# Queueing the output weight's splits, one batch's slot inputs and the joined products behind a chain that others wait for

## The chip, the cores and the metric

The kernel runs on 1 core of one Trainium2 chip. The metric is the device time of one execution in microseconds (us); lower is better. The engines are PE (TensorE, matrix products), DVE (VectorE), ACT (ScalarE), POOL (GpSimd) and SP (the queue that issues most DMAs); they run side by side, each in its own order, and wait for each other by semaphores.

## What is computed

Three parts follow each other on 4608 tokens (8 batches of 576) of width 512. `x` of a part is the output of the part before it.

```python
# 1: attention, 8 heads of 64, softmax over blocks at or before one's own block of 64
x = softmax(mask(q @ k.T / 8)) @ v
# 2: soft mixture of 8 experts with 4 slots each
logits = x @ phi                                   # 4608 x 32
slot_input = softmax(logits, over tokens).T @ x    # 32 x 512
slot_out[e] = relu(slot_input[e] @ w1[e]) @ w2[e]
x = softmax(logits, over slots) @ slot_out
# 3: bilinear layer
out = ((x @ m2_w1) * (x @ m2_w2)) @ m2_w3 @ m2_w_out
```

## The kernel before

**Attention** (class `Attn`) works on 32 pairs of heads, four to a batch. The order of its instructions on all engines comes from a planner (`Plan`), which gives each operation a duration, a due time and the operations that it waits for; `Attn.run` (L770) writes them out in that order. While it runs, POOL, DVE and ACT also unpack pieces of the bilinear layer's weights (`background`); the output weight `w_out` then lies in the tile `wO`. Of each batch's 576 tokens the planner also makes the logits, the combine weights (`cT`, which go to the array `cs` in memory by `cTd`) and that batch's share of the slot inputs (`S`, added up in `SS` by `SSu`).

**The tail of attention** (`push_tail`, L600) does the same for the last batch, out of the planner. It is a list of small steps: logits (L630), their transposes (L639) and scaling on DVE (L642, L645), natural-order tokens (`x_nat`, L682, L684), the softmax over tokens (`disp_max`, L689 and the exponentials L545 to L555), its transposes (L698), the sum over all batches (`slot_sum`: `tot` L719, its transpose L721, and a chain of eight operations on one partition, L726 to L733), the slot inputs (`slot_in`, L577, L579, L706), the scale `rl` (`slot_share`, L738, L740) and the transposed, scaled slot inputs `siT` (`slot_T`, L710 to L714). Between them stand small products of zeros (`warm`, L45), which only keep PE busy. With `siT` the experts can begin.

**The experts and the joined weight** (`Rest.run`). Since `m2_w3 @ m2_w_out` doesn't depend on the tokens, it is computed as one matrix `W` of 1024 x 512 in 192 joined products (L908), which are put between the experts' steps in portions: `MM[k]` says how many go out at step k, and the last call, step `STEPS` = 28, sends out all that are left. For each product both factors are split into a high and a low part (`split`, L862): a cast to the high part, and a subtraction for the low part. For `wO` and the first two pieces of `w3` (`convert(0)`, `convert(1)`) both are done on POOL; for the other fourteen pieces of `w3`, which are unpacked by four DVE operations (`narrow`, L808 to L816) and one of ACT (L812), the cast is ACT's and the subtraction POOL's. An expert e takes its first layer (L993, tile `h`), a copy `hs` by ACT (L1002), two transposes `hTp` (L1011), the rectified copy by ACT (L1012) and its second layer (L1021, tile `so`).

**The factors' chain.** After the last expert: copy `so`, sum and transpose it (`sumT`, L950), multiply by `m2_w1` and `m2_w2` (`ab`, L1062), copy, transpose (`abT`, L1069) and copy again (L1076). From these two factors DVE and ACT make the products of slot pairs in eight groups (L1088 to L1096, tile `g_stage`), and POOL one small part (L1099 to L1101); PE multiplies them by `W` (L1110, L1116) into `H` (L1120). **The final stage** (`final`) multiplies pairs of combine weights by `H`: 36 tiles of 13 matmuls (L1213, L1215).

In `Attn.run` the order of the planner's operations is kept as written. From `push_tail` on, a scheduler orders each engine's instructions, except in the manual region from the experts on, where PE's and SP's order is as written; `tc.issue_after(x)` keeps what is inside from being put ahead of x. The lines around the change:

```python
self.tail.extend([*logits[:2], sum_t, *logits[2:], *lts, *(F(x_late, c) for c in range(3)), F(fill, 1), disp_max, F(x_late, 3), F(x_late, 4),
                  F(fill, 2), disp_nat, slot_sum, F(fill, 3), slot_in, slot_share, F(fill, 4), slot_T, F(fill, 5)])
```

## Time and profile before

| | |
|---|---|
| three timed runs | 603.77 us median (602.77 to 604.93) |
| the profiled execution | 603.69 us, span of its instructions 601.9 us |
| PE busy | 573.4 us (95% of the span) |
| DVE, ACT, POOL busy | 396.2, 318.7, 343.3 us |
| granted PE clock, mean over the span | 0.971 |

The profile is of one execution. A stretch (start:end, in us from the first instruction) has the busy time of each engine, the share of full speed that PE's clock was granted, and the share of time that the DMA engines were busy. A row of a timeline has the start, the time taken, the engine, the line of the kernel, the operation, the tile that is written <- the tiles that are read, and in brackets how long the engine stood idle before it and whose result it then waited for. A matmul of unsplit 32-bit values (L630, L993, L1021) shows as two in the trace, one of split values (L908, L1110, L1213) as one. The attention part ends at about 343 us, the tail at 369, the experts at 444, the factors' chain at 456, and the final stage begins at 489.

### The profile page before, as it was taken

Reading aid. Unit: us, or ns where it says so; the run is one execution under the profiler, and the core shown is the slowest. Engines: PE = TensorE matmul, PEld = TensorE weight load, DVE = VectorE, ACT = ScalarE, POOL = GpSimd, SP = SyncE. Lnnn points to the kernel's source line nnn. Section 1 sums busy time; section 2 is a strip of 40 time slices with the busy share of each in tenths; the row PEclk is TensorE's granted clock in tenths of the full one; section 3 lists DMA queues with packets and bytes.
Section 4 is the critical chain, followed back from the end, with each engine's and each line's share of the span. In section 5 each row is a group of like instructions: output and inputs, shape, how many; then the busy total and the mean of one; then the engine's idle time right before and its main releaser. Section 6 shows DMA issues by size and latency. Waiting matters only on the chain.

```text
span 601.9 us, 13924 instructions
## 1 busy us (share of the span) xinstructions
PE 573.4 (95%) x5467; PEld 421.6 (70%) x5467; DVE 396.2 (66%) x701; ACT 318.7 (53%) x615; POOL 343.3 (57%) x256
## 2 busy tenths in 40 slices
PE   6999999999999999999999959999996999999997
PEld 3777777777777777776777635556562778888885
DVE  5648769788788798797884276735416995564550
ACT  4556477586675784874865522432532265445351
POOL 6587987878859969878768490411542032133230
PEclk8699999999999999999999987999997999999999
DMA  7243683754555647447436556999943026657642
GB/s 244 81 158 103 207 306 101 237 165 141 169 194 164 184 143 227 148 132 231 132 112 219 206 220 247 399 429 423 423 167 107 1 85 192 207 173 246 200 145 105
DMA packets 41113, 116.96 MB, mean 194 GB/s; under 512 B 7244, under 2 KB 17468, under 8 KB 38984
## 3 DMA queue, kind: packets, MB, share of 16 engines
q1 hardware_dynamic: 40868, 116.00, 56.1%
q8 instruction: 43, 0.70, 0.5%
q14 instruction: 22, 0.18, 0.1%
q10 hardware_dynamic: 180, 0.07, 0.0%
HBM read 105.75 MB, written 10.45 MB: 193 GB/s over the span
## 4 chain that ended last, share of the span: by engine, by line
PE 82%; DVE 9%; DMA 3%; ACT 3%; issue 2%; POOL 0%; ACTq 0%; DVEq 0%; POOLq 0%; SPq 0%
PE sc L371 18%; PE ops L1213 17%; PE pv L404 14%; PE wps L908 8%; PE sc L331 5%; PE pv L420 4%; PE h L993 3%; PE so L1021 2%; PE pv L528 2%; DVE bm L335 2%; DMA raw<-in_moe_w 2%; DMA raw<-in_qk 1%; PE ops L1215 1%; PE pv L471 1%; PE pv L577 1%
## 5 line engine op out<-in xcount | busy, mean ns | idle before, releaser
L335 DVE TENSOR_REDUCE bm<-sc 128x10 f32<-128x640 f32 (+2 forms) x128 | 122.5, 987 | 24.1 <-PE sc L331 20.3
L371 PE MATMUL sc<-set 64*128 64x320 f32 (+4 forms) x1152 | 116.8, 311 | 0.8 <-ACT PTa L379 0.3
L319 POOL TENSOR_TENSOR set<-raw,set 128x1152 fp32r<-128x1152 f32 x32 | 84.9, 2655 | 32.4 <-ACT set L312 31.0
L371 PEld LDWEIGHTS sc<-set 64*128 64x128 f32 x1152 | 90.7, 189 | 10.3 <-issue 3.8
L1213 PE MATMUL ops<-H,Ph 128*128 128x512 f32 x288 | 90.7, 395 | 0.9 <-DVE H L1120 0.9
L1188 POOL TENSOR_TENSOR Pl<-rot,Ph 128x384 fp32r<-128x384 f32 x24 | 31.0, 1311 | 92.5 <-ACT Ph L1186 92.5
L389 POOL TENSOR_TENSOR acc<-PTa,PTb 128x640 f32<-128x640 f32 x32 | 49.7, 1554 | 32.2 <-ACT PTb L379 25.0
L1213 PEld LDWEIGHTS ops<-H,Ph 128*128 128x128 f32 x288 | 54.3, 189 | 14.7 <-DVE H L1120 1.3
L371 PE MATMUL sc<-shift 64*128 64x320 f32 (+4 forms) x384 | 59.7, 305 | 0.0
L1213 PE MATMUL ops<-H,Pl 128*128 128x512 f32 x144 | 56.9, 395 | 0.0
L331 PE MATMUL sc<-set 64*128 64x320 f32 (+4 forms) x384 | 47.4, 330 | 4.1 <-ACT set L312 2.5
L1216 ACT COPY o<-ops 128x512 f32<-128x512 f32 x36 | 21.0, 587 | 57.0 <-PE ops L1215 56.7
L908 PE MATMUL wps<-wo,w 128*128 128x512 f32 x192 | 50.8, 406 | 0.0
L389 POOL TENSOR_TENSOR acc<-acc,PTc 128x640 f32<-128x640 f32 x31 | 48.2, 1556 | 2.4
L379 ACT ACTIVATE PTa<-sc 128x1024 f32<-128x1024 f32 x32 | 32.8, 1025 | 30.8 <-PE sc L371 28.3
L379 ACT ACTIVATE PTc<-sc 128x640 f32<-128x640 f32 (+1 forms) x64 | 41.7, 652 | 11.1 <-PE sc L371 10.2
L908 PEld LDWEIGHTS wps<-wo,w 128*128 128x128 f32 x192 | 34.1, 188 | 16.8 <-issue 10.8
L867 POOL TENSOR_TENSOR w<-f,w 128x512 fp32r<-128x512 f32 x14 | 18.1, 1290 | 46.7 <-ACT w L866 40.5
L404 PE MATMUL pv<-PTc,v 128*64 128x256 f32 (+1 forms) x256 | 44.0, 422 | 0.4 <-ACT xT L532 0.2
L462 POOL TENSOR_TENSOR xT<-xT,shift 128x576 f32<-128x576 f32 x28 | 39.0, 1422 | 3.9 <-DMA shift<-rr 3.7
L413 ACT COPY xT<-pv 128x256 f32<-128x256 f32 (+1 forms) x64 | 25.2, 397 | 28.2 <-PE pv L408 23.1
L379 ACT ACTIVATE PTb<-sc 128x1024 f32<-128x1024 f32 x32 | 32.8, 1024 | 11.3 <-PE sc L371 10.0
(248 smaller groups left out, 1133.1 us busy)
## 6 DMA issues: line engine op xcount, KB each, us to landing
win<-in_moe_w SPq DMA_DIRECT2D x16, 2048.0 KB
raw<-in_qk SPq DMA_DIRECT2D x32, 576.0 KB
v<-in_v SPq DMA_DIRECT2D x32, 320.0 KB
rot<-cs SPq DMA_DIRECT2D x48, 192.0 KB
out<-o SPq DMA_DIRECT2D x11, 768.0 KB
raw<-in_moe_w SPq DMA_DIRECT2D x16, 512.0 KB
shift<-rr SPq DMA_DIRECT2D x56, 144.0 KB
w3raw<-in_w3T SPq DMA_DIRECT2D x14, 512.0 KB
```

The costliest lines, as they stand in the source:

```text
L319: self.nc.gpsimd.tensor_tensor(lo, self.raw.pop(n), hi.bitcast(F32), op=ALU.subtract)
L331: self.nc.tensor.matmul(ps[:, h, o:o + kn], lhsT=qh[r, q0:q0 + 128], rhs=kh[r, k0:k0 + kn], start=True, stop=True)
L335: self.nc.vector.tensor_reduce(self.bmb[n % 2][:, :, o:o + m // 64], self.st.pop(("M", n, i))[:, :, 0:m].rearrange("p h (n k) -> p h n k", ...
L371: self.nc.tensor.matmul(ps[:, h, o0:o0 + w], lhsT=lt[r, k] if i < 3 else lt[r], rhs=rt[r, q0:q0 + w], start=i == 0, stop=i == 3)
L379: self.nc.scalar.activation(out=out, in_=ps[:, :, 0:sum(g[3] for g in self.UNITS[u])], func=AF.Exp, scale=SCALE)
L389: eng.tensor_tensor(acc[:, :, lo:hi], a, b, op=ALU.add)
L404: mm(ps[64 * h:64 * h + 64, q0 - lo:q1 - lo], lhsT=v[:, 128 * j + 64 * h:128 * j + 64 * h + 64], rhs=pt[:, h, o:o + q1 - q0], start=j == 0 ...
L413: self.nc.scalar.copy(self.xTb[b % 2][:, p, lo:hi], self.st.pop(("V", n, part))[:, 0:hi - lo])
L462: self.nc.gpsimd.tensor_tensor(x, x, self.rb[:, i], op=ALU.mult)
L908: nc.tensor.matmul(p, lhsT=a[:, o], rhs=b, start=c + i == 0, stop=c == 7 and i == 2)
L1188: eng.tensor_tensor(Pl[:, k], p, Ph[:, k].bitcast(F32), op=ALU.subtract)
L1213: nc.tensor.matmul(ps, lhsT=a[:, k, r], rhs=b[:, k], start=n == 0, stop=False)
```

## The change

It has three parts, besides line numbers that grow by up to four behind them.

1. The steps `S`, `SSu`, `cT`, `cTc` and `cTd` of the next-to-last batch are no longer written out where the planner puts them, but collected in `self.late` and written out in the tail behind the three steps that transpose and scale the last batch's logits (`lts`).
2. The splits of `wO` and of the first two pieces of `w3` wait for the copy of `rl` (`keep["shared"]`), the cast is ACT's instead of POOL's (`early` is gone), and each piece of `w3` is split ahead of the four pieces of `wO` that it meets.
3. `MM` changes at steps 21 and 24 to 27: the sum of all portions is 178 instead of 192, so that 14 joined products are left for the last call, which stands behind the factors' copies (L1076).

```diff
--- before.py
+++ after.py
@@ -32,7 +32,7 @@
 HP = False
 CT = (1, 2)
 STEPS = 28
-MM = (0, 5, 4, 13, 5, 4, 14, 5, 4, 13, 5, 4, 14, 5, 4, 13, 5, 4, 14, 5, 4, 13, 5, 4, 14, 4, 4, 4)
+MM = (0, 5, 4, 13, 5, 4, 14, 5, 4, 13, 5, 4, 14, 5, 4, 13, 5, 4, 14, 5, 4, 14, 5, 4, 2, 2, 4, 3)
 EPS = 1e-9
 
 SP = 640
@@ -241,7 +241,7 @@
         self.keep = keep
         self.raw, self.v = {}, {}
         self.m, self.mt, self.PT, self.acc, self.st = {}, {}, {}, {}, {}
-        self.tail = deque()
+        self.tail, self.late = deque(), []
 
         self.ident = keep["ident"]
         self.bmb = [self.const.tile([128, 2, 45], F32, name=f"bm{i}") for i in range(2)]
@@ -737,7 +737,7 @@
             ps = pst("rl")
             nc.tensor.matmul(ps[:, 0:1], lhsT=st["w"], rhs=ident[0:1, 0:1], start=True, stop=True)
             st["rl"] = tl([128, 1], "rl")
-            nc.scalar.copy(st["rl"], ps[:, 0:1])
+            self.keep["shared"] = nc.scalar.copy(st["rl"], ps[:, 0:1]).ins
 
         F = lambda f, *a: (lambda: f(*a))
         logits = [F(logit, g, i) for g in range(2) for i in range(2)]
@@ -750,7 +750,8 @@
             if WARM[i]:
                 warm(nc, self.keep, pst("warm"), WARM[i])
 
-        self.tail.extend([*logits[:2], sum_t, *logits[2:], *lts, *(F(x_late, c) for c in range(3)), F(fill, 1), disp_max, F(x_late, 3), F(x_late, 4),
+        late = [F(getattr(self, "op_" + name), n, slot) for name, n, slot in self.late]
+        self.tail.extend([*logits[:2], sum_t, *logits[2:], *lts, *late, *(F(x_late, c) for c in range(3)), F(fill, 1), disp_max, F(x_late, 3), F(x_late, 4),
                           F(fill, 2), disp_nat, slot_sum, F(fill, 3), slot_in, slot_share, F(fill, 4), slot_T, F(fill, 5)])
 
         def rest(tile, psum):
@@ -770,6 +771,9 @@
         self.constants()
         with self.tc.manual_schedule(engines={getattr(mybir.EngineType, e) for e in ORDERED}):
             for (name, n), slot, idle in Plan(self.nb).order():
+                if n == self.nb - 2 and name in ("S", "SSu", "cT", "cTc", "cTd"):
+                    self.late.append((name, n, slot))
+                    continue
                 if idle > .5 and name[0] in "MmQ" and n < 2:
                     warm(self.nc, self.keep, self.pv_b[slot] if name == "mT" else self.sc_b[slot][:, 0], int(4.5 * idle - 1), 256)
                 f = getattr(self, "op_" + name, None)
@@ -859,11 +863,8 @@
         self.nc.sync.dma_start(out=v, in_=self.io["moe_w1" if first else "moe_w2"][e].rearrange("p (c f) -> p c f", c=4 if first else 8))
         self.loaded.append(v)
 
-    def split(self, hi, lo, src, early=False):
-        if early:
-            self.nc.gpsimd.tensor_copy(hi, src)
-        else:
-            self.nc.scalar.copy(hi, src)
+    def split(self, hi, lo, src):
+        self.nc.scalar.copy(hi, src)
         self.nc.gpsimd.tensor_tensor(lo, src, hi.bitcast(F32), op=ALU.subtract)
 
     def run(self, out):
@@ -894,7 +895,7 @@
             def convert(i):
                 t = self.narrow(None, raws.pop(i), self.tmp, ps_u) if i > 1 else self.wO[:, 8 + i]
                 pair = w3_tile(i, F32R, "w3")
-                self.split(pair[:, 0:512], pair[:, 512:1024], t, i < 2)
+                self.split(pair[:, 0:512], pair[:, 512:1024], t)
                 pairs[i] = pair[:, 0:512], pair[:, 512:1024]
 
             def w_rows():
@@ -958,12 +959,13 @@
             for i in range(2, 2 * W3B):
                 load(i)
             done[0] = 2 * W3B
-            for c in range(8):
-                t = wo.tile([128, 1024], F32R, name=f"wo{c}")
-                wos.append((t[:, 0:512], t[:, 512:1024]))
-                self.split(*wos[c], self.wO[:, c], True)
-                if c % 4 == 0:
-                    convert(c // 4)
+            with tc.issue_after(keep["shared"]):
+                for c in range(8):
+                    if c % 4 == 0:
+                        convert(c // 4)
+                    t = wo.tile([128, 1024], F32R, name=f"wo{c}")
+                    wos.append((t[:, 0:512], t[:, 512:1024]))
+                    self.split(*wos[c], self.wO[:, c])
             done[1] = 2
             w_steps(0)
```

The instruction order on each engine, before and after, at the three places that matter. The lines of the changed kernel lie up to four lines further down. Numbers behind a name tell tiles of one name apart: `pv_117` and `pv_118` are two PSUM banks of the tail, `sc_116` holds two more; `xT_130` is the next-to-last batch, `xT_131` the last; `c` are combine weights.

PE in the tail, before:

```order
L630 MATMUL sc_116<-xT_131,phib 64x288 x2
L577 MATMUL pv_118<-xT_130,d 32x512 x4
L579 MATMUL pv_118<-xT_130,d 32x128 x4
L510 MATMUL pv_117<-ident,c 128x128
L511 MATMUL pv_117<-ident,c 32x128
L630 MATMUL pv_117<-xT_131,phib 64x288 x2
L630 MATMUL pv_118<-xT_131,phib 64x288 x2
L630 MATMUL pv_117<-xT_131,phib 64x288 x2
L639 MATMUL pv_118<-ident,Lg 128x128 x4
L639 MATMUL sc_116<-ident,Lg 128x128 x4
```

PE in the tail, with the change:

```order
L630 MATMUL sc_116<-xT_131,phib 64x288
L630 MATMUL pv_118<-xT_131,phib 64x288 x2
L630 MATMUL sc_116<-xT_131,phib 64x288
L630 MATMUL pv_117<-xT_131,phib 64x288 x4
L639 MATMUL pv_118<-ident,Lg 128x128 x4
L639 MATMUL sc_116<-ident,Lg 128x128 x4
L510 MATMUL pv_117<-ident,c 128x128
L511 MATMUL pv_117<-ident,c 32x128
L577 MATMUL pv_118<-xT_130,d 32x512 x4
L579 MATMUL pv_118<-xT_130,d 32x128 x4
```

The next-to-last batch's slot inputs (L577, L579) and combine transposes (L510, L511) moved from between the logits to behind the first two transposes of the logits. Further down in the same order the transpose of `tot` (L721) moved from ahead of `slot_in` to behind it and behind nine of the sixteen small warming products that follow it. DVE's order there moved in step: `SSu` (L589) stands behind the second scaling of the logits, and the last two scalings of tokens (L684) ahead of L539 and of L555.

ACT between the copy of `rl` and the first expert's transposed copy, before:

```order
L740 COPY rl<-sc_116 128x1
L656 ACTIVATE last_C<-last_C 128x160
L812 ACTIVATE m_5255<-w3raw 128x512
L1002 COPY hs<-h 128x256
L866 CAST w_5262<-f_5260 128x512
```

The same with the change, from the ninth of ten casts behind the copy of `rl` on:

```order
L867 CAST wo_5248<-wO 128x512
L867 CAST wo_5251<-wO 128x512
L816 ACTIVATE m_5255<-w3raw 128x512
L656 ACTIVATE last_C<-last_C 128x160
L867 CAST w_5262<-f_5260 128x512
L816 ACTIVATE m_5299<-w3raw 128x512
L1004 COPY hs<-h 128x256
```

Ten casts, a cast of a piece of `w3` that DVE has to unpack first, and a second preparing step (L816) now stand ahead of `hs`. On POOL ten subtractions in a row answer to the ten casts, in their order.

PE behind the factors' transposes, before:

```order
L908 MATMUL wps<-wo_5248,w_5850 128x512
L908 MATMUL wps<-wo_5251,w_5850 128x512 x3
L1069 MATMUL abT<-ident,abs 128x128 x4
L1116 MATMUL Hp_5998<-wO,g_stage 32x512 x8
L1110 MATMUL Hp_5994<-g_stage_5914 128x512 x2
```

And with the change:

```order
L909 MATMUL wps<-wo_5233,w_5781 128x512 x2
L909 MATMUL wps<-wo_5236,w_5781 128x512
L1071 MATMUL abT<-ident,abs 128x128 x4
L909 MATMUL wps<-wo_5236,w_5781 128x512 x2
L909 MATMUL wps<-wo_5242,w_5851 128x512 x3
L909 MATMUL wps<-wo_5245,w_5851 128x512 x3
L909 MATMUL wps<-wo_5248,w_5851 128x512 x3
L909 MATMUL wps<-wo_5251,w_5851 128x512 x3
L1118 MATMUL Hp_5998<-wO,g_stage 32x512 x8
```

Fourteen joined products moved from ahead of `sumT`, `ab` and `abT` to behind `abT`. The copy and the split of the last row of `W` by ACT and POOL moved behind POOL's small slot products with them.

## Rows read from the trace of the kernel before

**Rows 1.** The page, part 4: shares of the span in the chain that ended last.
```profile
PE 82%; DVE 9%; DMA 3%; ACT 3%; issue 2%; POOL 0%; ACTq 0%; DVEq 0%; POOLq 0%; SPq 0%
```

**Rows 2.** Stretches: start:end, length; busy us (instructions) of PE, PEld, DVE, ACT, POOL; clock; DMA.
```profile
352.40:355.80 3.40, 1.80 (x11) 1.20 (x12) 3.26 (x7) 0.30 (x1) 3.40 (x4) 1.00 0.50 195
...
355.80:359.20 3.40, 2.68 (x18) 2.06 (x16) 2.50 (x6) 1.60 (x7) 3.40 (x4) 0.51 0.00 0
...
380.30:444.40 64.10, 63.88 (x498) 37.00 (x497) 29.71 (x43) 22.59 (x48) 20.35 (x16) 1.00 0.95 398
...
455.70:460.50 4.80, 0.00 (x0) 0.00 (x0) 4.34 (x9) 1.54 (x6) 3.77 (x4) 0.76 0.74 228
...
460.50:489.00 28.50, 27.52 (x116) 19.42 (x116) 25.99 (x48) 10.53 (x20) 2.48 (x2) 0.92 0.03 11
...
489.00:601.90 112.90, 109.31 (x467) 87.83 (x467) 55.83 (x91) 50.27 (x104) 28.50 (x22) 1.00 0.54 178
```

**Rows 3.** Timeline of PE, 342 to 369 us: start, us, engine, line, operation, tiles.
```profile
344.42 1.07 PE L577 MATMUL pv<-xT,d 128*32 128x512 f32 x8
...
346.52 1.91 PE L630 MATMUL pv<-xT,phib 128*64 128x288 f32 x12 [0.45 <-ACT cT L516]
...
361.04 0.37 PE L721 MATMUL pv<-ident,tot 128*1 128x128 f32 x1 [2.56 <-DVE tot L719]
...
362.90 1.94 PE L577 MATMUL sc<-xT,d 128*32 128x512 f32 x8
```

**Rows 4.** Timeline of DVE, 340 to 372 us.
```profile
345.85 0.75 DVE L589 SCALAR_TENSOR_TENSOR SS<-SS,dal,pv 128x512 f32<-128x512 f32 x1 [1.80 <-PE pv L579]
...
349.13 0.69 DVE L642 TENSOR_TENSOR lr<-pv,r 128x512 f32<-128x512 f32 x1 [2.53 <-PE pv L639]
...
357.95 3.04 DVE L719 SCALAR_TENSOR_TENSOR tot<-Ls 128x1 f32<-128x1 f32 x1
```

**Rows 5.** Timeline of POOL, 340 to 365 us.
```profile
351.14 9.83 POOL L867 TENSOR_TENSOR wo<-wO,wo 128x512 fp32r<-128x512 f32 x8
```

**Rows 6.** Timeline of PE, 442 to 490 us.
```profile
444.36 4.37 PE L908 MATMUL wps<-wo,w 128*128 128x512 f32 x18
...
460.53 3.64 PE L1116 MATMUL Hp<-wO,g_stage 128*32 128x512 f32 x16 [4.87 <-DVE g_stage L1093]
...
476.50 11.04 PE L1110 MATMUL Hp<-W,g_stage 128*128 128x512 f32 x48
...
488.98 0.50 PE L1213 MATMUL ops<-H,Ph 128*128 128x512 f32 x1 [0.95 <-DVE H L1120]
```

**Rows 7.** Timelines of ACT, 366 to 385 and 442 to 470 us.
```profile
367.01 0.16 ACT L740 COPY rl<-sc 128x1 f32<-128x1 f32 x1 [4.57 <-PE sc L738]
...
372.90 0.37 ACT L1002 COPY hs<-h 128x256 f32<-128x256 f32 x1 [2.23 <-issue]
...
373.90 0.67 ACT L812 ACTIVATE m<-w3raw 128x512 bf16<-128x512 f32 x1
...
444.98 1.14 ACT L1046 CAST g_stage<-wO 128x512 fp32r<-128x512 f32 x2
```

**Rows 8.** One stretch of the tail, in the columns of rows 2.
```profile
361.00:363.75 2.75, 2.48 (x16) 1.37 (x20) 2.21 (x7) 0.31 (x1) 0.00 (x0) 0.50 0.00 0
```

**Rows 9.** Timeline of PE, 369 to 445 us.
```profile
374.07 0.38 PE L1011 MATMUL hTp<-ident,hs 128*128 128x128 f32 x2
...
375.31 1.92 PE L1021 MATMUL so<-win,win 128*32 128x512 f32 x16
```

**Rows 10.** Timelines of POOL and DVE in the final stage, 486 to 530 us.
```profile
492.27 2.49 POOL L1188 TENSOR_TENSOR Pl<-rot,Ph 128x384 fp32r<-128x384 f32 x2 [5.53 <-ACT Ph L1186]
...
492.51 1.36 DVE L1191 TENSOR_TENSOR half<-half 32x384 f32<-32x384 f32 x1
```

**Rows 11.** Timelines of DVE and ACT between 442 and 490 us.
```profile
456.98 1.47 DVE L1089 TENSOR_TENSOR g_stage<-AB,AB 128x512 f32<-128x512 f32 x1 [0.39 <-ACT AB L1076]
...
464.29 0.58 ACT L1135 COPY H<-Hp 128x512 f32<-128x512 f32 x1 [3.11 <-PE Hp L1116]
```

## The prediction

> **What bounds the kernel now.** I read the chain of waits first. PE carries 82% of it [rows 1], so a gain has to make PE do less, wait less, or run at the higher of its two clocks. The second view is the table of stretches. Two stretches in the second half show PE neither busy nor fast. From 352.4 to 359.2 us the last batch's tail runs: PE is busy 1.80 of 3.40 us, and then the granted clock is at the lower of its two levels (1.2 of 2.4 GHz; 0.51). From 455.7 to 460.5 PE does nothing at all, and the clock falls to the lower level again (0.76 as a mean, 0.92 for the stretch behind it) [rows 2]. From 489.0 to the end PE is busy 109.31 of 112.90 us: the final products, 36 tiles of a fixed length. The change leaves them as they are, so I treat their 113 us as fixed and ask when they start.
>
> The third view is the timeline of single engines in those two stretches. In the tail the next-to-last batch's slot inputs (L577) and combine transposes stand between the logits (L630): the block starts at 344.42 and the logits go on at 346.52, after a wait for the copy of cT [rows 3]. On DVE a sum of one element per partition (L719, `tot`) takes 3.04 us [rows 4], and it ends at 360.99, when POOL's eight subtractions of the output weight's splits end (351.14 + 9.83 = 360.97) [rows 5]. Both operands of `tot` lie in SBUF, as do POOL's; the DVE operations around it, with an operand in PSUM, are not stretched. PE waits 2.56 us for it [rows 3]. In the second stretch 14 + 4 + 4 + 4 joined products (L908) run before or between the links of the factors' chain (so, sumT, ab, abT); after abT PE waits 4.87 us for POOL and DVE to make the first slot products [rows 6].
>
> **The change, part by part.** The sum is made against the profiled execution's own 603.69 us (span 601.9), which is 0.1 below the median of the three runs.
>
> *A. The tail, up to the copy of rl (367.01) [rows 7].* Taking the slot inputs and cT out from between the logits frees up to 2.1 us (346.52 - 344.42). The last logit still has to wait for a copy out of its bank, so I take 1.6 of 2.1. The slot inputs' update on DVE, 0.75 us (L589), now stands between DVE's logit steps, which start at 349.13 [rows 4]: that gives back 0.7, so 0.9 is left. With no POOL streak beside it `tot` costs nothing: 3.0 more. The last batch's slot inputs (L577, 362.90 [rows 3]) then start 3.9 sooner, at 359.0. But PE's order now has the transpose of `tot` behind them and behind nine of the small warming products. What was hidden beside them is laid bare: from that transpose to the end of the reciprocal 2.75 us [rows 8], with the last multiply and a tiny matmul some 3.4. At the lower clock the slot inputs take about 2.4 (1.94 for their first part) and nine warming products about 1.0: 359.0 + 2.4 + 1.0 + 3.4 = 365.8, a gain of 1.2. At the higher clock (1.07 instead of 1.94 [rows 3], warming at half price) the same sum gives 358.4 + 1.3 + 0.5 + 3.4 = 363.6, a gain of 3.4. The clock fell at about 355.8, after slices in which PE was half busy. The moved slot inputs add 1.3 us of work to just those slices and the 2.56 us wait goes, so it lies nearer to the higher level. I take **-2.6**.
>
> *B. The splits, now behind rl.* ScalarE gets ten casts that GpSimd had, and GpSimd's ten subtractions wait for them. GpSimd has nothing else to do here, so it gains nothing by losing its casts. ACT's queue is what costs: the first expert's copy of hs now stands behind ten casts, two preparing steps, and a cast that needs DVE's unpacked weight. Two casts take 1.14 us, so ten take 5.5; then 0.67 (preparing), 0.69 (DVE's last step, as a 128x512 operation in [rows 4]), 0.57 (cast), 0.67, 0.37 (hs) [rows 7] and 0.16 for rl itself: hs is ready 8.6 us after rl starts. PE's transposes of hs stood 7.06 after it (374.07 - 367.01 [rows 9]). That is **+1.5** on the path, since products, the second layer's matmuls and the next expert's first layer queue behind those transposes on PE. The five products ahead of them need only two splits. The last split is done at 0.7 + 10 x 1.23 = 13.0 after rl. PE asks for it after the transposes, the second layer (1.92) and sixteen products of 0.243, about 14.5 after rl: covered, with 1.5 us to spare; without that cover the excess would go on the path. The ends for B are +0.5 (the clock is low in h, so less is exposed) and +2.5.
>
> *DVE beside the ten subtractions.* The last batch's combine weights (L653 and L663, two operands in SBUF) now run while POOL subtracts. In the final stage such an operation takes 1.36 us while two POOL subtractions of 2.49 run back to back [rows 10]: it got its turn between the two. At one turn each, L653 waits at most 1.2 and is done before ACT needs it, so I cost it at nothing. The Trainium skill's page "Advanced Engine Details and Errata" (VectorE Performance Modes) says that GpSimd instructions and two-port Vector instructions block each other, because the second port is shared, and "GPSIMD Engine Reference" (Key points) adds Vector instructions with two SBUF inputs. The pages do not say who gets the next turn; with one turn the sum is as here, with a wait for the whole streak it is the second rival below. `tot` waited over two boundaries between POOL operations, the other case waited over none.
>
> *C. The joined products behind the factors' chain.* Fourteen of 192 products move from before abT to behind it, at 4.37 / 18 = 0.243 us each: abT ends 3.4 sooner. One more product stands before the last expert's chain: 0.2 back, so -3.2. The moved products then fill 3.4 of the 4.87 us hole, PE keeps the higher clock, and the sixteen matmuls of L1116 cost 1.8 instead of 3.64 [rows 6]. PE's work from abT (460.53 - 4.87 = 455.66 today) to the final products is then 3.4 + 1.8 + 96 x 0.23 + 0.5 = 27.8 us, against 33.3 now (488.98 - 455.66), so PE is no longer what holds this stage: DVE is. DVE is busy 25.99 of 28.50 us there [rows 2]: at most 2.5 to win. ACT's copy (L1135) waits 3.11 us for L1116 and holds back the cast that DVE needs; that goes. The first slot product's 1.47 us, half of it POOL's last split beside it [rows 11], only moves, as the split comes later. I take 1.8 of 2.5, with ends 0 and 3.3. **C = -3.2 - 1.8 = -5.0** (-3.2 to -6.5).
>
> Sum: -2.6 + 1.5 - 5.0 = -6.1, so 603.69 - 6.1 = **597.6 us**.
>
> **The rivals.**
> *The slot-product stage keeps its length* (C = -3.2): DVE is busy for nine tenths of it, so the filled hole may only turn into waiting further on. -2.6 + 1.5 - 3.2 = -4.3, 599.4 us.
> *DVE is passed over (slower than before).* L653 waits for the whole streak of ten subtractions, as `tot` did, with DVE's unpacking of the next weight, ACT's cast and hs queued behind it. The streak ends at rl + 13.0; four unpacking steps of 0.7, a cast, a preparing step and hs bring it to 17.4, 10.3 later than now: -2.6 + 10.3 - 5.0 = +2.7, 606.4 us. For it stands `tot` [rows 4, 5]. Against it stand [rows 10], and that `tot` is the one such case. The sign turns where L653 is passed over by five or more subtractions.
> *The clock eats the tail's gain.* A at its low end (-1.2) and one more stretch at the lower clock, some 1.7 us, while PE waits for hs: -1.2 + 3.2 - 5.0 = -3.0, 600.7 us. Against it: PE's longest waits there become shorter.
> *The expert weights arrive no sooner.* DMA is at a share of 0.95 from 380.3 to 444.4 [rows 2], so what A and B gain (-1.1) may be lost: 598.7 us. Against it, PE has next to no idle time there now, and each load is released by PE, so it moves along.
> *The order is not what runs* or all terms cancel: 603.8 us.
>
> **Chances.** Forecast 0.60, its own range 594.5 to 600.0; slot products keep their length 0.10; clock 0.08; weights 0.08; passed over 0.10; no change 0.04. The range 593.8 to 601.2 takes in the first four and leaves out the last two and the ends. A measurement here can tell about 0.3% (1.8 us) from no change: faster 0.85, same 0.05, slower 0.10.
>
> **What would show it.** `tot` at about 0.2 us instead of 3.04; rl near 364.4; hs's copy late behind ACT's casts with a wait of PE of one to two us before the first hTp; L653 not longer than 1.5 us; no PE wait of over 1 us between abT and L1116, and no lower clock there; abT's end to the final products 31.5 us. It is wrong if L653 or hs is late by five us or more, if rl does not come sooner, or if the final products still start 33 us behind abT.

## The result, and the profile after

The changed kernel takes 597.82 us (median of 11 runs, 595.34 to 601.79), the kernel before 603.65 (11 runs, 602.12 to 605.03): a ratio of 0.9911, 95% interval 0.9890 to 0.9933, or 5.4 us less (4.0 to 6.6). The ratio is taken over all runs; the two medians differ by 5.8. The profiled execution of the changed kernel took 599.57 us (span 597.8), 1.75 above its median; before it was 603.69 (span 601.9). Line numbers are up to four higher than before, and in the experiments they move by some more.

Cut at four starts, which one row each of PE's timeline gives (the last batch's first logits, the second expert's first layer h(1), the end of abT, the second final product), the two executions compare so:

| us | logits to h(1) | h(1) to abT's end | abT's end to the final products | final products to the end |
|---|---|---|---|---|
| before | 36.66 | 75.34 | 33.31 | 112.92 |
| after | 35.34 | 72.65 | 31.59 | 114.47 |

The first three stretches gain 1.3, 2.7 and 1.7 us. The fourth, which I had treated as fixed, loses 1.55. Together the executions differ by 4.2 us behind the first logits, so the account below explains 4.2 of the 5.4.

**The tail.** The timeline of PE, changed kernel:

```profile
358.60 1.06 PE L577 MATMUL sc<-xT,d 128*32 128x512 f32 x8
...
360.33 0.27 PE L721 MATMUL pv<-ident,tot 128*1 128x128 f32 x1
...
363.31 0.35 PE L738 MATMUL sc<-ident,w 1*128 1x1 f32 x2 [2.32 <-DVE w L733]
364.43 1.92 PE L713 MATMUL pv<-sel,sn 128*128 128x32 f32 x8 [0.77 <-DVE sn L710]
366.82 3.64 PE L995 MATMUL h<-win,siT 128*32 128x256 f32 x32 [0.47 <-DVE siT L714]
...
372.76 0.44 PE L1013 MATMUL hTp<-ident,hs 128*128 128x128 f32 x2 [0.86 <-ACT hs L1004]
```

The timeline of DVE:

```profile
347.43 0.69 DVE L642 TENSOR_TENSOR lr<-pv,r 128x512 f32<-128x512 f32 x1 [3.31 <-PE pv L639]
...
349.96 0.74 DVE L589 SCALAR_TENSOR_TENSOR SS<-SS,dal,pv 128x512 f32<-128x512 f32 x1
...
357.94 0.16 DVE L719 SCALAR_TENSOR_TENSOR tot<-Ls 128x1 f32<-128x1 f32 x1
...
366.94 1.44 DVE L653 TENSOR_TENSOR last_C<-last_L,cmx 128x160 f32<-128x160 f32 x1
```

And that of ACT:

```profile
363.70 0.16 ACT L740 COPY rl<-sc 128x1 f32<-128x1 f32 x1 [2.12 <-PE sc L738]
...
371.26 0.62 ACT L867 CAST w<-f 128x512 fp32r<-128x512 f32 x1 [1.40 <-DVE f L820]
371.79 0.65 ACT L816 ACTIVATE m<-w3raw 128x512 bf16<-128x512 f32 x1
372.35 0.35 ACT L1004 COPY hs<-h 128x256 f32<-128x256 f32 x1
```

`tot` is 0.16 us instead of 3.04 [rows 4], the slot inputs start at 358.60 instead of 362.90 and at the higher clock [rows 3], and `rl` comes at 363.70 instead of 367.01 [rows 7]. But `tot`'s transpose now stands behind the slot inputs and nine warming products, and PE waits 2.32 us for the chain from `tot` to `w`. hs comes 8.65 us after rl.

**The end of the span.** The table of stretches, in the columns of [rows 2]:

```profile
356.95:363.80 6.85, 4.06 (x51) 2.57 (x48) 3.57 (x11) 1.39 (x8) 0.00 (x0) 1.00 0.36 130
363.80:370.60 6.80, 5.70 (x41) 3.57 (x42) 4.50 (x8) 6.07 (x13) 6.15 (x5) 0.50 0.82 332
...
451.75:480.65 28.90, 27.98 (x128) 20.96 (x127) 27.35 (x50) 10.09 (x21) 5.18 (x5) 1.00 0.25 75
480.65:483.30 2.65, 0.52 (x2) 0.19 (x1) 2.62 (x5) 2.60 (x6) 1.04 (x1) 0.99 0.23 74
483.30:486.70 3.40, 3.37 (x8) 2.73 (x9) 3.34 (x7) 0.66 (x2) 0.00 (x0) 0.51 0.71 213
```

PE's timeline has these rows there:

```profile
451.49 3.43 PE L909 MATMUL wps<-wo,w 128*128 128x512 f32 x14
455.84 1.50 PE L1118 MATMUL Hp<-wO,g_stage 128*32 128x512 f32 x12 [0.92 <-POOL g_stage L1103]
...
480.67 0.50 PE L1215 MATMUL ops<-H,Ph 128*128 128x512 f32 x1
483.33 0.80 PE L1215 MATMUL ops<-H,Ph 128*128 128x512 f32 x1 [2.16 <-DVE H L1122]
```

And DVE's:

```profile
477.57 1.96 DVE L1187 TENSOR_TENSOR rot<-rot,crep 128x384 f32<-128x384 f32 x4
479.44 1.37 DVE L1193 TENSOR_TENSOR half<-half 32x384 f32<-32x384 f32 x1
480.75 1.80 DVE L1190 TENSOR_TENSOR Pl<-rot,Ph 128x384 fp32r<-128x384 f32 x2
482.58 1.89 DVE L1122 TENSOR_TENSOR H<-Hp,H 128x512 fp32r<-128x512 f32 x3
```

The fourteen products fill the hole behind abT (0.92 us of waiting instead of 4.87 [rows 6]), and the clock stays up until 483. Then PE is ready for H, and DVE isn't: it first makes the low parts of the first tiles' products. PE stands for 2.16 us (0.95 before [rows 6]), the granted clock falls to the lower level, and the final stage begins at half speed. In the page's chain (part 4) PE's share has fallen from 82% [rows 1] to 76%, and those of DVE and DMA have grown:

```profile
PE 76%; DVE 12%; DMA 6%; ACT 2%; issue 2%; POOL 0%; ACTq 0%; DVEq 0%; SPq 0%; POOLq 0%
```

### The profile page after: what moved, and what is told of

The parts are those of the page before. It is cut to its first block, busy times and chain, and to the rows that moved or that the text cites. A ratio compares the mean times of both kernels' runs of the same rounds, so it can differ in the third digit from the quotient of the medians.

```text
span 597.8 us, 13917 instructions
## 1 busy us (share of the span) xinstructions
PE 570.2 (95%) x5467; PEld 421.5 (71%) x5467; DVE 397.4 (66%) x701; ACT 323.3 (54%) x625; POOL 335.9 (56%) x246
## 4 chain that ended last, share of the span: by engine, by line
PE 76%; DVE 12%; DMA 6%; ACT 2%; issue 2%; POOL 0%; ACTq 0%; DVEq 0%; SPq 0%; POOLq 0%
PE ops L1215 17%; PE sc L371 16%; PE pv L404 13%; PE wps L909 6%; PE sc L331 5%; PE pv L420 3%; DVE bm L335 3%; PE so L1023 3%; DMA raw<-in_moe_w 2%; PE pv L528 2%; PE h L995 2%; DMA raw<-in_qk 2%; PE ops L1217 1%; DMA win<-in_moe_w 1%; DVE g_stage L1092 1%
## 5 line engine op out<-in xcount | busy, mean ns | idle before, releaser
L371 PEld LDWEIGHTS sc<-set 64*128 64x128 f32 x1152 | 90.6, 189 | 10.1 <-issue 4.2
L1215 PE MATMUL ops<-H,Ph 128*128 128x512 f32 x288 | 91.9, 400 | 2.2 <-DVE H L1122 2.2
L1190 POOL TENSOR_TENSOR Pl<-rot,Ph 128x384 fp32r<-128x384 f32 x24 | 28.7, 1216 | 92.3 <-ACT Ph L1188 92.3
L331 PEld LDWEIGHTS sc<-set 64*128 64x128 f32 x384 | 30.8, 195 | 11.9 <-issue 4.7
```

The source lines that it names most:

```text
L331: self.nc.tensor.matmul(ps[:, h, o:o + kn], lhsT=qh[r, q0:q0 + 128], rhs=kh[r, k0:k0 + kn], start=True, stop=True)
L371: self.nc.tensor.matmul(ps[:, h, o0:o0 + w], lhsT=lt[r, k] if i < 3 else lt[r], rhs=rt[r, q0:q0 + w], start=i == 0, stop=i == 3)
L1190: eng.tensor_tensor(Pl[:, k], p, Ph[:, k].bitcast(F32), op=ALU.subtract)
L1215: nc.tensor.matmul(ps, lhsT=a[:, k, r], rhs=b[:, k], start=n == 0, stop=False)
```

## The experiments

The stretches are those of the table above, each from the one profiled execution of its run. The last batch's logits start at 341.3 to 344.8 us in them; that shifts the whole time of single executions, but not these stretches. The first stretch itself scatters by 1 us (u_mm and the changed kernel have the same edits up to there, and take 34.34 and 35.34).

| run | median us (runs) | ratio to before, 95% | logits to h(1) | to abT's end | to final products | to the end |
|---|---|---|---|---|---|---|
| after | 597.82 (11) | 0.9911 (0.9890 to 0.9933) | 35.34 | 72.65 | 31.59 | 114.47 |
| u_late | 596.46 (6) | 0.9891 (0.9866 to 0.9916) | 33.14 | 72.30 | 31.59 | 113.32 |
| u_split | 597.65 (6) | 0.9908 (0.9881 to 0.9934) | 34.35 | 72.20 | 31.59 | 114.49 |
| u_mm | 601.33 (12) | 0.9963 (0.9942 to 0.9984) | 34.34 | 75.73 | 32.98 | 112.36 |
| only_joined | 598.51 (6) | 0.9929 (0.9911 to 0.9948) | 35.62 | 72.21 | 31.59 | 114.52 |
| tot_tt | 596.81 (1) | none | 34.50 | 72.20 | 31.58 | 113.35 |
| tot_first | 595.04 (5) | 0.9857 (0.9834 to 0.9880) | 30.86 | 72.25 | 31.57 | 114.48 |
| hs_first | 596.53 (6) | 0.9887 (0.9869 to 0.9906) | 34.28 | 72.40 | 31.56 | 113.91 |
| fin_order | 596.55 (6) | 0.9888 (0.9869 to 0.9907) | 35.28 | 72.66 | 29.84 | 114.09 |
| joined | 594.83 (4) | 0.9860 (0.9833 to 0.9888) | 31.82 | 72.28 | 29.83 | 114.12 |
| warmer | 593.44 (4) | 0.9839 (0.9810 to 0.9867) | 31.79 | 73.50 | 29.85 | 114.15 |
| more_behind | 596.58 (6) | 0.9896 (0.9867 to 0.9925) | 32.30 | 71.50 | 33.13 | 113.58 |
| joined_no_late | 593.26 (6) | 0.9832 (0.9792 to 0.9873) | 32.63 | 72.44 | 29.83 | 114.12 |

### Each part undone by itself

**u_late: part 1 undone.**

```diff
-                if n == self.nb - 2 and name in ("S", "SSu", "cT", "cTc", "cTd"):
+                if False:
```

> The changed kernel with part 1 undone: the next-to-last batch's slot inputs and cT stand where the planner puts them, between the last batch's logits. My sum: 1.6 us of PE's time come back between the logits and 0.7 us leave DVE behind them, so the copy of rl comes 0.9 us later and the time is 597.8 + 0.9 = 598.7 us; tot stays at about 0.2 us, since nothing of GpSimd's runs beside it. Rival 1: the slot inputs cost PE the same at either place, so the time stays within 0.5 us of 597.8. Rival 2: the full 2.1 us come back and the lower clock with them, 600 us or more.

The median came out 1.4 us below the changed kernel, where all theories had it level or above. The two intervals overlap, so the sign isn't proven by the times; the trace says where it would come from. PE's timeline:

```profile
357.90 0.42 PE L721 MATMUL pv<-ident,tot 128*1 128x128 f32 x1
...
361.52 0.35 PE L738 MATMUL sc<-ident,w 1*128 1x1 f32 x2 [0.15 <-DVE w L733]
...
364.20 1.93 PE L995 MATMUL h<-win,siT 128*32 128x256 f32 x32 [0.47 <-ACT wo L867]
...
368.36 0.44 PE L1013 MATMUL hTp<-ident,hs 128*128 128x128 f32 x2 [0.87 <-ACT hs L1004]
...
370.96 1.92 PE L1023 MATMUL so<-win,win 128*32 128x512 f32 x16 [1.23 <-ACT win L1014]
```

Without part 1 the transpose of `tot` stands ahead of the slot inputs. The chain to `w` runs beside them, PE waits 0.15 us for it instead of 2.32, and the clock stays at its higher level through h(0): 1.93 us instead of 3.64. So part 1 had a side effect that I had counted as 3.4 us of bare chain, but not as a choice of order that could be undone.

**u_split: part 2 undone.** `split` has its `early` form back, and the loop over `wO` its old order:

```diff
-    def split(self, hi, lo, src):
-        self.nc.scalar.copy(hi, src)
+    def split(self, hi, lo, src, early=False):
+        if early:
+            self.nc.gpsimd.tensor_copy(hi, src)
+        else:
+            self.nc.scalar.copy(hi, src)
...
-            with tc.issue_after(keep["shared"]):
-                for c in range(8):
+            for c in range(8):
...
```

> The changed kernel with part 2 undone: the ten first splits are GpSimd's alone again and start as soon as they can, before rl. My sum: tot waits for GpSimd's subtractions again (about 3 us instead of 0.16, rl 2.5 to 3 us later), and hs no longer stands behind ten casts (hs 2 us sooner after rl): +3.0 - 2.0, so 598.8 us. Rival: tot's 3 us had nothing to do with the subtractions, tot stays at 0.2 and the time falls by the 2 us of hs, 595.8 us.

The time stayed where it was. `tot` again stands beside GpSimd's subtractions, but it waits for one of them only: it ends at 358.34, and 352.15 + 5 x 1.23 = 358.30. DVE's row and POOL's:

```profile
357.66 0.68 DVE L719 SCALAR_TENSOR_TENSOR tot<-Ls 128x1 f32<-128x1 f32 x1
```

```profile
352.15 9.86 POOL L871 TENSOR_TENSOR wo<-wO,wo 128x512 fp32r<-128x512 f32 x8
```

And with part 1 in place `tot` has time: its transpose comes behind the slot inputs either way, at 360.05 here, 1.7 us after `tot` is done. From the multiply by w to h(1) this run took 14.77 us (377.82 - 363.05), the changed kernel 15.78 (379.09 - 363.31): **the splits cost 1.0 us on the path**, with the clock low in h(0) in both.

**u_mm: part 3 undone.**

```diff
-MM = (0, 5, 4, 13, 5, 4, 14, 5, 4, 13, 5, 4, 14, 5, 4, 13, 5, 4, 14, 5, 4, 14, 5, 4, 2, 2, 4, 3)
+MM = (0, 5, 4, 13, 5, 4, 14, 5, 4, 13, 5, 4, 14, 5, 4, 13, 5, 4, 14, 5, 4, 13, 5, 4, 14, 4, 4, 4)
```

> The changed kernel with part 3 undone: no joined product behind the factors' chain. My sum: abT 3.2 us later and the slot-product stage 1.8 us longer, PE waiting some 4.9 us behind abT as before: 597.8 + 5.0 = 602.8 us. Rival: the stage from abT to the final products keeps its length and only the 3.2 us come back, 601.0 us.

601.33 us: 3.5 by the medians, 3.1 by the ratios ((0.9963 - 0.9911) x 603.65), so the rival's 601.0 rather than my 602.8. The stretches say why. Without part 3 abT ends 3.1 us later after h(1), and the slot-product stage is 1.4 longer, as I had expected; but the final stage is 2.1 shorter. PE's timeline of this run has the hole back, and only a short wait for H:

```profile
457.32 3.60 PE L1118 MATMUL Hp<-wO,g_stage 128*32 128x512 f32 x16 [4.86 <-DVE g_stage L1095]
...
485.44 0.50 PE L1215 MATMUL ops<-H,Ph 128*128 128x512 f32 x1 [1.11 <-DVE H L1122]
```

From abT's end to the end of the span it takes 145.34 us, the changed kernel 146.06, the kernel before 146.23. **In these executions part 3 gains nothing clear behind abT.** In two other executions with part 3 (u_late, tot_tt) PE waits as long for H, but the clock stays up, and it takes 144.91 and 144.93 us: the fall of the clock costs some 1.1 of what is lost there. The table of stretches of u_late has this row at the start of its final stage:

```profile
479.90:483.30 3.40, 3.26 (x13) 2.38 (x14) 3.34 (x7) 0.68 (x3) 0.00 (x0) 1.00 0.75 214
```

**only_joined: parts 1 and 2 undone together** (the two diffs above).

> Part 3 alone (parts 1 and 2 undone). My sum, A - B as predicted: parts 1 and 2 are worth 1.1 us together, so 597.8 + 1.1 = 598.9 us, a ratio to before of about 0.992. Rival 1 (parts 1 and 2 each win what the other wins as well: the runs with one of them undone stood at 0.989 and 0.991): undoing both costs 2 to 3.5 us, 600 to 601 us, ratio 0.994 to 0.997. In the trace tot stands beside GpSimd's eight subtractions again: theory of the turn, it ends with the next subtraction to end; theory of the streak, it ends with the last of the eight.

598.51 us, near my number (598.9) and below the rival's 600 to 601. The ratio's interval (0.9911 to 0.9948) still takes in the rival's lower end of 0.994, and it overlaps that of the changed kernel. Here `tot` waits to the end of the last subtraction again: 351.84 + 9.85 = 361.69, and 358.65 + 3.06 = 361.71. It passed two boundaries between subtractions (359.23 and 360.46). DVE and POOL:

```profile
358.65 3.06 DVE L719 SCALAR_TENSOR_TENSOR tot<-Ls 128x1 f32<-128x1 f32 x1
```

```profile
351.84 9.85 POOL L871 TENSOR_TENSOR wo<-wO,wo 128x512 fp32r<-128x512 f32 x8
```

**tot_tt: another form for `tot`**, in the kernel of u_split.

```diff
-            nc.vector.scalar_tensor_tensor(tot, Ls[:, 1:2], 0.25, Ls[:, 0:1], op0=ALU.mult, op1=ALU.add)
+            nc.vector.tensor_scalar(tot, Ls[:, 1:2], 0.25, None, op0=ALU.mult)
+            nc.vector.tensor_tensor(tot, tot, Ls[:, 0:1], op=ALU.add)
```

> As the run above with part 2 undone, but tot is made by two DVE instructions, a multiply by 0.25 and a sum of two operands, instead of one that does both. Theory 1 (a turn is what counts): each of the two waits for at most one of GpSimd's subtractions, 1.4 us or less, as the last batch's combine weights did in the changed kernel. Theory 2 (a small DVE operation is passed over as long as GpSimd has work): one of the two ends when the last of the eight subtractions ends, and takes 2.5 us or more. Theory 3 (neither is stretched): it is the form of the single instruction that waits, both stay under 0.3 us.

One execution, 596.81 us. DVE:

```profile
357.49 0.15 DVE L719 TENSOR_SCALAR tot<-Ls 128x1 f32<-128x1 f32 x1
357.68 0.56 DVE L720 TENSOR_TENSOR tot<-tot,Ls 128x1 f32<-128x1 f32 x1
```

The sum of two operands waits to the next boundary (0.56 us), as theory 1 says. But u_split, which the form was to be compared with, did the same with the old form, so this run doesn't tell the forms apart.

### What the changed kernel still gave away

**tot_first: `tot`'s transpose ahead of the slot inputs.**

```diff
-            self.inputs(ps, st["d"], xT)
+            with self.tc.issue_after(st["tt"]):
+                self.inputs(ps, st["d"], xT)
...
-                nc.tensor.transpose(ps[0:1, 128 * i:128 * i + 128], t, ident)
+                st["tt"] = nc.tensor.transpose(ps[0:1, 128 * i:128 * i + 128], t, ident).ins
...
-            if WARM[i]:
+            with self.tc.issue_after(st["tt"]) if i == 4 else nullcontext():
```

> The changed kernel with the transpose of tot put ahead of the last batch's slot inputs on PE, and the sixteen warming products behind them. Theory: part 1 pushed that transpose behind the slot inputs and nine warming products, which laid a chain of eight small DVE and ACT operations bare; PE's wait of 2.3 us for w falls to 0.5 or less, the multiply by w starts 1.7 us sooner, and since the clock then stays at its higher level through siT and h(0), another 0.8 to 1.7 us come: 594.4 to 596.1 us, ratio 0.985 to 0.988. Rival: hs on ACT sets the pace, so the gain before it becomes a longer wait of PE for hs: within 0.5 us of 597.8.

Confirmed: ratio 0.9857, 3.3 us below the changed kernel, and the two intervals don't meet. The wait for w falls to 0.95 us, not to 0.5, and h(0) is still at the lower clock for most of its time. PE:

```profile
358.69 0.35 PE L739 MATMUL pv<-ident,w 1*128 1x1 f32 x2 [0.95 <-DVE w L734]
...
361.37 3.24 PE L996 MATMUL h<-win,siT 128*32 128x256 f32 x32 [0.38 <-DVE siT L715]
```

**hs_first: hs ahead of the unpacking on ACT.** `w_steps(0)` goes, and no piece of `w3` is unpacked before step 2, which waits for the first rectified copy:

```diff
-                    while done[1] < done[0] and done[1] * 12 < done[2] + AHEAD:
+                    while k > 1 and done[1] < done[0] and done[1] * 12 < done[2] + AHEAD:
...
-                w_steps(3 * e + 2)
+                with tc.issue_after(relu) if e == 0 else nullcontext():
+                    w_steps(3 * e + 2)
```

> The changed kernel with the first expert's copy hs ahead of the unpacking of the third piece of w3 on ACT (the ten casts stay ahead of it). Theory B: of the 8.6 us from rl to hs the ten casts alone take 5.3, and h(0) ends 6.8 us behind rl; without the two preparing steps and the cast hs starts when h(0) ends, hTp starts 0.9 us sooner and PE's wait for hs goes: -0.9, 596.9 us. Rival: h(1) starts no sooner, since the third piece of w3 now comes later and its products wait: 597.8 us or more.

596.53 us, ratio 0.9887; the difference from 0.9911 is within the intervals. In the trace PE's wait for hs is gone:

```profile
371.17 0.38 PE L1012 MATMUL hTp<-ident,hs 128*128 128x128 f32 x2
```

And from the multiply by w to h(1) it takes 14.72 us (377.43 - 362.71): 1.06 less than in the changed kernel, the whole cost of the splits that u_split showed. It was the two preparing steps and the cast behind the ten casts that cost, not the ten casts.

**fin_order: DVE makes H's first low part ahead of the low parts of the products.**

```diff
-                    eng.tensor_tensor(Pl[:, k], p, Ph[:, k].bitcast(F32), op=ALU.subtract)
+                    with after(u, 8 + k) if eng is nc.vector else nullcontext():
+                        eng.tensor_tensor(Pl[:, k], p, Ph[:, k].bitcast(F32), op=ALU.subtract)
```

(`after(u, i)` is `tc.issue_after(self.fences[i])` for u = 0, else nothing; the subtraction for the small fifth part of the products stands behind fence 11 likewise.)

> The changed kernel with DVE's order changed where the final stage begins: the first low part of H ahead of the low parts of the first tiles' products (nothing is left out). Theory: PE's wait of 2.2 us for H was DVE's order, not DVE's work; the first subtraction of H starts when ACT has copied its high part, the stage from abT's end to the final products falls from 31.6 to 29.7 us, and the clock stays at its higher level in the final stage (112.4 to 113.0 us instead of 113.3 to 114.5): -1.9 to -3.4, 594.4 to 595.9 us, ratio 0.985 to 0.988. Rival: the low parts of the products come later by the same amount and PE waits for them instead: within 0.5 us of 597.8.

The stage from abT's end falls to 29.84 us and the clock stays at 1.00, both as expected. The final stage is 114.09 and not 112.4 to 113: the parts of H now come one by one at DVE's pace. PE:

```profile
480.71 0.49 PE L1220 MATMUL ops<-H,Ph 128*128 128x512 f32 x1 [0.41 <-DVE H L1122]
481.71 0.51 PE L1220 MATMUL ops<-H,Pl 128*128 128x512 f32 x1 [0.51 <-DVE Pl L1194]
```

From abT's end to the end it is 2.1 us less than in the changed kernel (143.93 for 146.06). By the ratios it is 1.4, short of the forecast 1.9 to 3.4, and the two intervals overlap.

**joined: these three edits together.**

> The three edits tot_first, hs_first and fin_order together in the changed kernel. Theory: tot_first (ratio 0.9857) and fin_order (0.9888 against 0.9911) act in different stages and add up; hs_first adds nothing here, since in tot_first PE no longer waited for hs: 597.8 - 3.2 - 1.4 = 593.2 us, ratio 0.983 to 0.985. Rival: the weights of the later experts set the pace and what the tail gains is lost before abT: 595 us or more, with the stretch from h(1) to abT longer than 72 us.

594.83 us, 4 runs. In the trace both gains are there (3.5 us up to h(1), 2.1 behind abT), and the stretch between isn't longer (72.28 us for 72.65), which speaks against the rival. The median is still level with tot_first alone, 1.6 above my sum; with intervals of 0.2 to 0.3% on each side the times don't say more.

**warmer: 34 warming products instead of 16, and hs behind eight casts**, in the kernel of joined. `WARM[4]` is 34, and the loop over `wO` stops after c = 5; the other two splits are issued behind hs.

> As the run above, with 34 instead of 16 warming products between the slot inputs and the multiply by w (18 more at 0.066 us each fill PE's wait of about 1 us for w) and with hs behind eight of the ten casts instead of all ten. Theory: the clock stays at its higher level, h(0) takes 1.9 us instead of 3.2, and hs and its transposes follow 0.5 to 1.1 us sooner: 0.5 to 1.3 us below the run above, ratio 0.981 to 0.983. Rival: GpSimd's subtractions, 12.7 us for ten, then set when the thirteen products of step 3 end, and the time stays within 0.5 us of the run above.

593.44 us, ratio 0.9839: just above the forecast 0.981 to 0.983, and its interval overlaps that of joined. The forecast's mechanism didn't come. PE's wait for w is gone, but the clock falls all the same, at 364.5 us: h(0) takes 3.45. The timeline of PE:

```profile
359.87 2.06 PE L45 MATMUL pv<-zeros 128*128 128x128 bf16 x34
361.88 0.36 PE L739 MATMUL pv<-ident,w 1*128 1x1 f32 x2
363.01 1.08 PE L714 MATMUL sc<-sel,sn 128*128 128x32 f32 x8 [0.77 <-DVE sn L711]
364.47 3.45 PE L998 MATMUL h<-win,siT 128*32 128x256 f32 x32 [0.38 <-DVE siT L715]
```

Up to h(1) it is level with joined (31.79 and 31.82 us), so its lower median is not explained by this edit.

**more_behind: 28 products behind abT** instead of 14, in the kernel of joined (`MM[18]` and `MM[21]` are 7).

> As the run with the three edits, with 28 instead of 14 joined products behind the factors' chain (seven each taken from steps 18 and 21). Theory: abT comes up to 3.4 us sooner, but behind it PE now has 31.2 us of work where DVE needs about 29.7, so the stage grows by 1.5 to 2.5 and the time falls by 1 to 2 us, ratio 0.979 to 0.982. Rival 1: the weights of the last experts set the pace (DMA share 0.95 there), abT comes no sooner and the stage grows: 1.5 to 2.5 us slower than the run with the three edits. Rival 2: both cancel, within 0.5 us.

Rival 1: 596.58 us, 1.8 above joined, though the two intervals still overlap. abT comes only 0.8 us sooner after h(1), because PE now waits for the experts' weights, and the stage behind it grows by 3.3. PE:

```profile
433.25 1.93 PE L995 MATMUL h<-win,siT 128*32 128x256 f32 x32 [1.85 <-DMA win<-in_moe_w]
...
438.13 1.92 PE L1024 MATMUL so<-win,win 128*32 128x512 f32 x16 [0.46 <-DMA win<-in_moe_w]
...
447.75 6.65 PE L910 MATMUL wps<-wo,w 128*128 128x512 f32 x28
```

**joined_no_late: part 1 undone, with hs_first and fin_order.**

> The changed kernel with part 1 undone, and with the edits hs_first and fin_order (tot_first isn't needed: without part 1 the transpose of tot stands ahead of the slot inputs anyway). Question: is part 1 worth anything once its side effect on tot's transpose is mended? Theory: from the last batch's logits to the multiply by w it stays at 18.7 us as in u_late, the waits for hs (0.9) and for the rectified copy (1.2) go, and the final stage gains 1.4: 596.5 - 2.1 - 1.4 = 593.0 us, level with the three edits that keep part 1 (ratio 0.983 to 0.987). Rival: part 1 is worth the 1.3 us by which the trace of tot_first is shorter in that stretch (17.4 against 18.7): 1.3 us slower than those, 596 us, ratio 0.988.

593.26 us, the theory's number. The tail is 0.8 us shorter with part 1 (31.82 in joined, 32.63 here), less than the scatter of 1 us in that stretch, and the times don't show it: 0.9832 (0.9792 to 0.9873) and 0.9860 (0.9833 to 0.9888). So part 1 isn't shown to be worth anything. This version and warmer are the best, some 10 us below the kernel before and 4 below the change.

## Why the prediction was right, and where it wasn't

The total (597.6) was within 0.3 us of the median, and that is in part luck. By the profiled executions the change gave 4.2 us (1.3 up to h(1), 2.9 behind it) and not 6.1, which makes 599.5; the profiled execution took 599.57, and the median lies 1.8 below it. Three things were wrong or missing: the second half of C, the credit for `tot`, and the low clock behind A's wait.

*Parts 1 and 2 in sum (A + B = -1.1).* It agrees, but the gain is no larger than the scatter. Up to h(1) the executions with both parts take 35.34, 34.34 and 35.28 us (after, u_mm, fin_order), those with neither 36.66 and 35.62 (before, only_joined): means of 34.99 and 36.14, a gain of 1.15. By the times it is 1.1 (only_joined to after, intervals overlapping) or 2.2 (before to u_mm).

*A (-2.6 to rl).* Undersized: from the first logits to the multiply by w 22.93 us became 19.56, a gain of 3.4, my end at the higher clock (18.55 in u_mm). That end has a flaw of its own: it starts the slot inputs at 358.4, where the steps ahead of it give 359.0, and no row stands for the 0.6. They started at 358.60. The steps were those of the text: the first logit step 1.7 sooner, SSu's 0.74 given back, `tot` at 0.16, 3.4 us from `tot`'s transpose to rl. What I didn't see: that last 3.4 us is not the price of part 1 but of PE's order behind it: in tot_first PE's wait for w falls from 2.32 to 0.95 us. And behind that wait the clock is low, from 363.8 to 370.6, which the forecast of A, ending at rl, left out.

*That A's 3 us for `tot` come from part 2.* Wrong as an attribution. With part 2 undone the time stays (u_split), since `tot` then waits for one boundary only and part 1 has its transpose later. With part 1 undone the subtractions are still gone (u_late). Undoing either alone costs nothing that the times show, so the 3 us can't be credited to one of them. That part 1 alone would also hide a wait of 3 us is argued, not shown: in u_split the wait was 0.5 us.

*B (+1.5).* hs came at rl + 8.65 as reckoned (8.6), though ten casts at 1.14 us for two would be 5.7 and not 5.5; they took 5.3. On the path it cost 1.0 us (u_split, hs_first), within +0.5 to +2.5. PE waited 0.86 us for hs, and not at all for the last split (13.0 us after rl reckoned, 13.4 measured). In joined_no_late, with hs sooner, the cover of 1.5 us that I had named was used up and PE waited 0.26 us for a split:

```profile
374.42 0.96 PE L909 MATMUL wps<-wo,w 128*128 128x512 f32 x3 [0.26 <-POOL wo L868]
```

*DVE beside the ten subtractions.* L653, L661 and L663 took 1.44, 1.30 and 1.41 us, one turn each; the rival of the long hold fell for them.

*C (-5.0).* The step that failed is its second half, "I take 1.8 of 2.5", together with "I treat their 113 us as fixed". The 3.2 us before abT came (3.1 against u_mm). The stage behind it also shrank, 33.31 to 31.59 where I had 31.5. But PE's earlier arrival turned into a longer wait for H (2.16 us for 0.95), the clock fell behind it, and the final stage, which is not fixed, lost what had been won: abT's end to the end is 146.06 us instead of 146.23. The rival "the slot-product stage keeps its length" had the right size of C, in the wrong place: that stage did shrink, and the one behind it grew. C measured: -3.1 us by the times (u_mm to after), 2.4 to 2.9 by the stretches (against u_mm and the kernel before), where I had -5.0. By the profiled executions the whole change is worth 4.1 us; the timed runs give 5.4, and their interval begins at 4.0.

*DMA.* That the expert weights would not hold it up was right for 14 products; with 28, and everything ahead of them shorter, they did (more_behind).

## What to carry to other kernels

When work is moved to fill a hole, follow the engine past the hole to the next thing it waits for, and ask what that producer does first: here DVE's order, not its load, then set the start of the last stage. When a block is moved out of a list, look at which small instruction of another chain now queues behind it. And two edits that can remove the same wait must not be counted twice; undo each alone before crediting either.

## What the runs showed of the hardware

*The clock after a wait.* In seven profiled executions PE waited 2.1 to 2.2 us for H just ahead of the final stage. In five of them (after, u_split, only_joined, tot_first, hs_first) the granted clock fell to 0.50 in the first microseconds of that stage, which then took 113.9 to 114.5 us; in two (u_late, tot_tt) it stayed at 1.00 and the stage took 113.3 to 113.4. In the other six executions of this study and in the kernel before, with waits of 0.2 to 1.1 us, it was 1.00 throughout. In the tail the same shows: in warmer PE had two waits of 0.77 and 0.38 us among small matmuls (busy 1.08 of 2.15 us), and h(0) then ran at 0.54; in u_late, with waits of 0.77 and 0.47 in the same places, it ran at 1.00. So much the same pattern may or may not cost the lower clock. That makes much of the 1 us by which the first stretches of the changed kernel and u_mm differ: the same ten warming products ran at the lower clock in the changed kernel (first row) and at the higher one in u_mm (second row).

```profile
355.04 1.27 PE L45 MATMUL sc<-zeros 128*128 128x128 bf16 x10
```

```profile
353.28 0.72 PE L45 MATMUL sc<-zeros 128*128 128x128 bf16 x10
```

*DVE beside GpSimd.* L653, L661 and L663 in three kernels (after, u_mm, u_late), `tot` in u_split and its sum in tot_tt ran beside back-to-back subtractions of GpSimd and took 0.56 to 1.44 us, one subtraction (1.27) and their own time at most. `tot` in the two kernels without parts 1 and 2 (before, only_joined) waited for the last of the eight, 3.04 and 3.06 us, over two boundaries. The form may count too: in tot_tt the multiply, a TENSOR_SCALAR of 128x1, took 0.15 us beside the same streak, while L661, a TENSOR_SCALAR of 128x5, took 1.13 to 1.30. The page "Advanced Engine Details and Errata" of the Trainium skill (VectorE Performance Modes) says that GpSimd instructions and two-port Vector instructions block each other over a shared port. The waits here look like that, but the traces don't show which port or mode an operation used. What lets an operation in at one boundary and not at the next stays open: `tot` in u_split and in the kernel before is the same instruction.
